# A sine table in 16-bit integers, a reciprocal by logarithm and exponential, and a reordered program

## The chip, the core and the metric

The kernel runs on one core of a Trainium2 chip. The metric is the device time of one execution in microseconds (us). The engines are PE (TensorE, matmuls, with its weight loads shown apart as PEld), DVE (VectorE), ACT (ScalarE), POOL (GpSimd) and SP (SyncE, which here issues all DMAs). Each engine takes its instructions in order; an instruction waits until what it reads is written and what it overwrites has been read.

## The reference

Two independent blocks on bf16 inputs of 2048 rows and 576 columns, whose results stand side by side in the output:

```python
# A: short filter, gate, long convolution over the sequence, gate
k_shift = sum_t k_pad[:, t:t+S, :] * shift_k[:, ks-1-t]      # ks = 4 taps
kv = k_shift * v
y = irfft(rfft(pad(kv)) * rfft(pad(ssm_k)))[:S]              # per column, length 2*2048
a = q * (y + kv * ssm_D)
# B: linear attention, 32 heads of 18
q, k, v = split(x @ wqkv); pq, pk = phi(q), phi(k)           # phi(t) = t+1 if t>0 else exp(t), plus 1e-6
kv = einsum("bhsd,bhse->bhde", pk, v); z = sum_s pk
b = (einsum(pq, kv) / (einsum(pq, z) + 1e-6)) @ wo
out = concat([a, b], axis=-1)
```

## The kernel before

Block A does the long convolution as a two-stage Fourier transform on PE. The 576 columns go in five chunks (four of 128 and one of 64). For each chunk and for the filter (letter h) and the signal (letter u): `s1` multiplies by the 16 tables of the sine matrices `G` (unit names h1, u1; eight matmuls, tile Ch or Cu), a DMA transpose turns the result (ht, ut; tile Cth, Ctu), and `s2` does the 16-point stage (h2, u2; tiles T for the filter and SU for the signal). `prod` multiplies the two complex spectra (pX, pT) and adds up planes (pA, pS). Where pA or pS has the engine letter N, it is left out and the inverse stage `i1` does the sum by eight more matmuls per half. `i1` writes V, and `i2` applies the transposed tables `F` and the gate q. `conv` (cv) is the short filter with the gate v, ahead of u1. The filter rows first get D added into their first column (hd) and are then transposed (hT): by PE and an eviction (letter D or A), or, for chunks 3 and 4 before the change, by a copy (letters a and p: tile hp) and a DMA transpose.

Block B transposes x (xd: by PE, or by DMA with the letter T), computes phi(k) for 16 groups of 128 rows (k) and phi(q) transposed (q, qt), sums x against phi(k) (G, zs), folds wv and wo in (kv, M), and divides by the denominator: den computes it and its reciprocal `rden`, bc and bt spread it over the columns of phi(q), o and ol are the last product with the output's DMA.

Nothing schedules this at run time. A string `ORDER` lists some 260 units by hand or by search, in the order in which they are written; each unit emits instructions to several engines, and every engine runs its own in that order. The letters behind a unit's dots choose the engine of an eviction or elementwise operation (A, D, P), and the digits behind the slash choose the PSUM banks (four pairs, 0 to 3) and buffer slots. A matmul into a bank waits until the bank's last reader is done. At the start: `io` makes small constants, `ix` the index of the sine tables on DVE (mp for the sine, mc for the cosine), `sin` turns them into G on ACT, `wu` issues matmuls on zeros ("warm_ps") before any data is there, Wj spreads the four filter taps over 128 partitions by matmuls from a row of ones (tile W_ps), dl and dc bring D. The index of an element is the product of (4k - 1) and (16p + s), taken modulo 8192.

Of the kernel before, what the change touches and what calls it, by code (L numbers as in the profile page):

```python
# [37 lines left out]
k.15/3 u1.0.1.0.A/2 hT.2.D/21 u1.0.0.1.A/0 u1.0.0.0.A/3 ht.1.1/0 cv.1.1.DD xd.1.T/1 k.13/2 h2.1.1.1.A/11 cv.1.2.DD
h2.1.1.0.A/0 q.3.1/3 h2.0.0.1.A/21 h2.0.0.0.A/2 ut.0.0/0 cv.1.3.DDP hl.3/0 q.3.0/0 q.1.0/1 u2.0.0.0.A/03 k.6/2
ut.0.1/1 k.7/0 u2.0.0.1.A/3 pX.0.0.D/0 qt.1/1 u2.0.1.0.A/12 u2.0.1.1.D/0 k.5/3 u1.1.1.0.A/12 kl.1 pT.0.0.D k.12/1  # L40
pX.0.1.D/1 u1.1.0.1.A/0 k.14/2 u1.1.1.1.A/3 ht.1.0/0 ql.0/1 cv.2.0.D u1.1.0.0.A/0 pT.0.1.D k.4/1 cv.2.1.DD
h1.2.1.1.A/03 pS.0.1.D pA.0.0.P ut.1.1/1 h1.2.1.0.A/2 hd.3 pA.0.1.D q.1.1/0 h2.1.0.0.A/33 h2.1.0.1.A/2 G.1/10
# [5 lines left out]
h1.3.1.1.A/1 u2.2.0.0.D/10 u2.2.0.1.A/2 ut.2.1/0 i1.1.1.1.A/03 cv.4.0.D i1.1.1.0.A/1 cv.4.1.DD den/0 lwo ht.3.1/1
hT.4.p/20 u2.2.1.1.A/02 i1.1.0.1.A/3 i1.1.0.0.A/1 M.2.A/2 M.3.A/3 i2.1.1/1 h2.3.1.1.A/12 cv.4.2.PP u2.2.1.0.A/0
i2.1.0/3 pX.2.0.P/1 u1.3.1.1.A/01 bc.2/20 u1.3.0.1.A/3 u1.3.0.0.A/1 bt/2 pA.2.0.N u1.3.1.0.A/3 M.1.A/0 ht.3.0/0  # L50
h2.3.1.0.D/1 h2.3.0.1.A/32 bc.0/30 h1.4.1.0.A/11 h1.4.0.1.A/2 st.0 h2.3.0.0.A/1 ut.3.0/1 pT.2.0.P bc.3/32 h1.4.1.1.A/0
M.4.A/1 M.0.A/3 bc.1/01 h1.4.0.0.A/2 pS.2.0.P u2.3.0.0.A/13 u2.3.0.1.A/2 pX.2.1.P/0 ut.3.1/0 ht.4.0/1 ql.1/1 pT.2.1.D
# [21 lines left out]
def _warm(tc, psum, K, n):  # L74

    nc = tc.nc
    zero = K.sm[:, 1984:2048].bitcast(BF)
    ps = psum.tile([128, 4, 128], FP32, name="warm_ps")
    for _ in range({'A': 5, 'B': 8, 'C': 7, 'D': 6}[n]):
        nc.tensor.matmul(ps[:], lhsT=zero, rhs=zero.unsqueeze(1).to_broadcast([128, 4, 128]), start=True, stop=True)  # L80


# [33 lines left out]
def _small(tc, cpool, slot, K):  # L116
    nc = tc.nc
    K.sm = slot([128, 2048], FP32, "sm")
    nc.vector.memset(K.sm[:, 1984:2048].bitcast(BF), 0.0)
# [2 lines left out]
    nc.gpsimd.iota(K.sm[:, 256:272], pattern=[[1, 16]], base=0, channel_multiplier=16,
                   allow_small_or_imprecise_dtypes=True)
# [3 lines left out]
    nc.vector.memset(K.negpi[:], -math.pi)  # L127
# [8 lines left out]
def _dft_index(tc, slot, K, part, h):

    nc = tc.nc
    b = slice(8 * h, 8 * h + 8)
    if part == 0:  # L140
        kap = K.sm[:, 128:256].unsqueeze(1).to_broadcast([128, 8, 128])
        sv = K.sm[:, 256 + 8 * h:264 + 8 * h].unsqueeze(2).to_broadcast([128, 8, 128])
        if not hasattr(K, 'mp'):
# [1 line left out]
        nc.vector.tensor_tensor(out=K.mp[:, b], in0=kap, in1=sv, op=ALU.mult)
        nc.vector.tensor_single_scalar(out=K.mp[:, b], in_=K.mp[:, b], scalar=8191, op=ALU.bitwise_and)
    else:
        if not hasattr(K, 'mc'):
            K.mc = slot([128, 2, 16, 128], I16, "mc")
        nc.vector.tensor_single_scalar(out=K.mc[:, 0, b], in_=K.mp[:, b], scalar=6144, op=ALU.add)  # L150
        nc.vector.tensor_single_scalar(out=K.mc[:, 1, b], in_=K.mc[:, 0, b], scalar=8191, op=ALU.bitwise_and)


# [90 lines left out]
def kernel(  # L244
# [134 lines left out]

    def shift_w(eng='A'):  # L380
        one = K.sm[0:97, 769:833].bitcast(BF)
        for i, e in enumerate({'A': 'AAA', 'D': 'DDD', 'M': 'ADA', 'N': 'DAD'}[eng]):
            d0, dn = 256 * i, min(256, D - 256 * i)
            ps = psum.tile([128, 1024], FP32, name="W_ps")
            for c0 in range(0, 4 * dn, 512):
                c1 = min(c0 + 512, 4 * dn)
                nc.tensor.matmul(ps[:, c0:c1], lhsT=one, rhs=K.Srow[:, 4 * d0 + c0:4 * d0 + c1], start=True, stop=True)
# [328 lines left out]
    def b_den():  # L716
# [17 lines left out]
        nc.vector.tensor_scalar(out=den, in0=den, scalar1=ez[:, 0:1], scalar2=None, op0=ALU.add)  # L734
        with nc.allow_low_precision(reason="the reciprocal is used as bf16"):
            nc.vector.reciprocal(out=B['rden'], in_=den)
# [88 lines left out]


    UNITS = {
        'xl': load_x, 'wm': one_w, 'lw': load_w, 'ls': load_shift, 'lz': zero_rows, 'Wj': shift_w, 'eps': eps_col,
        'dl': load_D, 'dc': turn_D, 'id': lambda: _ident(tc, cpool, K), 'io': lambda: _small(tc, cpool, slotx, K),
        'ix': lambda p, h: _dft_index(tc, slotx, K, p, h), 'iv': lambda: _w16_phase(tc, K),  # L830
        'iw': lambda: _w16_index(tc, K), 'wk': lambda: _w16_mask(tc, K), 'sin': lambda ri, h: _sine(tc, cpool, K, ri, h),
# [57 lines left out]
```

## Time and profile before

| what | us |
|---|---|
| median of three runs | 161.43 (161.31 to 162.2) |
| profiled execution, span from its first to its last instruction | 159.3 |
| PE busy in it | 147.6 |
| DVE busy | 139.8 |
| ACT busy | 128.4 |
| POOL busy | 65.2 |

The runs are timed from outside, the span from inside the profile, so the median stands 2.1 us over the span; the time of the profiled execution around its span is not shown apart. Busy means that at least one instruction of the engine was running. The end of a matmul is modelled and matmuls are pipelined, so the distance between starts says more of PE's rate than a matmul's length. In the rows that follow, a line number such as L532 is that of the kernel before; "x16" is the number of instructions, and what stands in square brackets is the idle time ahead of them and what ended it.

### The profile page before, as it was taken

To read this page: it belongs to the slowest core of one execution; us is meant where nothing else is said; L and a number is where in the kernel's file an instruction comes from. 1 tells how busy PE (TensorE), PEld (TensorE's weight loads), DVE (VectorE), ACT (ScalarE), POOL (GpSimd) and SP (SyncE) were. 2 spreads that over 40 slices of the span, in tenths; PEclk is the share of its full clock that TensorE was granted. 3 is DMA by queue.
4 is the path that set the end of the run, shared out by engine and by line. 5 is a ranking of instruction groups with operands and counts; after the bars stand their busy time and mean duration, and the time that the engine had idled before them with its cause. 6 is when DMAs were issued, how large, how long until landed. Compare 5 with 4: busy or idle time off the path is not lost.

```text
span 159.3 us, 4563 instructions
## 1 busy us (share of the span) xinstructions
PE 147.6 (93%) x1966; PEld 92.2 (58%) x1982; DVE 139.8 (88%) x170; ACT 128.4 (81%) x157; POOL 65.2 (41%) x67
## 2 busy tenths in 40 slices
PE   6799999999999999999998999999878999998990
PEld 1498564465734467467466568576445565677550
DVE  7978699899899999999899989998999999998420
ACT  7979996899997999959996956997999685786331
POOL 7407541806510970008100019589997077400000
PEclk9999999999999999999999999999999999999999
DMA  3999999990979999999999999684999999444282
GB/s 105 352 368 294 255 239 305 152 231 3 164 130 228 243 228 240 189 212 312 159 196 272 242 155 212 187 141 90 268 152 184 175 324 204 124 117 136 62 264 100
DMA packets 74171, 31.92 MB, mean 200 GB/s; under 512 B 52074, under 2 KB 73509, under 8 KB 74150
## 3 DMA queue, kind: packets, MB, share of 16 engines
q1 hardware_dynamic: 74150, 31.62, 91.7%
q8 instruction: 15, 0.25, 0.7%
q14 instruction: 6, 0.05, 0.1%
HBM read 14.97 MB, written 4.72 MB: 124 GB/s over the span
## 4 chain that ended last, share of the span: by engine, by line
PE 66%; POOL 12%; DVE 8%; DMA 6%; issue 3%; ACT 3%; SPq 0%; DVEq 0%; ACTq 0%; POOLq 0%
PE k_ps L451 12%; PE q_ps L460 11%; PE g_ps L659 6%; PE o_ps L776 6%; PE s_ps L532 6%; POOL X L567 5%; PE s_ps L555 5%; DMA Cth<-Ch 4%; PE i_ps L589 3%; POOL T L569 3%; PE hT_ps L511 2%; DMA pqT<-in_A_shift_k_dram 2%; PE xT_ps L337 2%; PE i_ps L602 2%; PE qt_ps L468 2%
## 5 line engine op out<-in xcount | busy, mean ns | idle before, releaser
L451 PE MATMUL k_ps<-wqk,xT 128*128 128x512 bf16 (+1 forms) x154 | 21.3, 282 | 0.3
L532 PEld LDWEIGHTS <-G 128*128 128x128 bf16 x320 | 17.4, 98 | 3.7 <-issue 3.4
L299 ACT ACTIVATE Cu<-s_ps 128x1024 bf16<-128x1024 f32 (+1 forms) x18 | 16.9, 978 | 2.1 <-DMA Cth<-Ch 1.4
L460 PE MATMUL q_ps<-xT,wqk 128*128 128x512 bf16 x78 | 18.2, 379 | 0.1
L451 PEld LDWEIGHTS <-xT 128*128 128x128 bf16 x160 | 11.4, 98 | 10.5 <-issue 0.5
L299 ACT ACTIVATE Ch<-s_ps 128x1024 bf16<-128x1024 f32 (+1 forms) x17 | 15.0, 928 | 3.0 <-PE s_ps L532 2.7
L299 ACT ACTIVATE ob<-o_ps 128x576 bf16<-128x576 f32 (+1 forms) x12 | 7.5, 636 | 11.3 <-PE o_ps L768 5.1
L299 ACT ACTIVATE V<-i_ps 128x1024 bf16<-128x1024 f32 x16 | 15.7, 1034 | 1.0 <-PE i_ps L589 1.0
L659 PE MATMUL g_ps<-pk,x_sb 128*128 128x65 bf16 (+1 forms) x124 | 16.3, 283 | 0.2
L299 ACT ACTIVATE T<-s_ps 128x1024 bf16<-128x1024 f32 x16 | 15.7, 1027 | 0.5 <-POOL at L490 0.5
L490 DVE TENSOR_TENSOR at<-at 128x2048 bf16<-128x2048 bf16 (+1 forms) x13 | 14.9, 1143 | 0.7 <-POOL at L489 0.3
L489 DVE TENSOR_TENSOR at<-k,Wj 128x2048 bf16<-128x2048 bf16 (+1 forms) x13 | 14.8, 1136 | 0.4 <-POOL at L490 0.4
L776 PE MATMUL o_ps<-wo_M,pqT 128*128 128x64 bf16 (+1 forms) x108 | 13.8, 283 | 0.5 <-issue 0.5
L444 DVE SCALAR_TENSOR_TENSOR pk<-pk,k_ps 128x576 bf16<-128x576 bf16 x16 | 11.8, 751 | 2.7 <-ACT pk L443 2.6
L299 ACT ACTIVATE SU<-s_ps 128x1024 bf16<-128x1024 f32 x14 | 14.1, 1029 | 0.0
L659 PEld LDWEIGHTS <-x_sb 128*128 128x128 bf16 x128 | 8.4, 97 | 8.7 <-issue 1.1
L460 PEld LDWEIGHTS <-wqk 128*128 128x128 bf16 x80 | 7.5, 98 | 9.1 <-issue 1.1
L443 ACT ACTIVATE pk<-k_ps,neg 128x576 bf16<-128x576 f32 x16 | 11.6, 745 | 1.2 <-PE k_ps L451 0.9
L604 DVE TENSOR_TENSOR q<-i_ps,q 128x1024 bf16<-128x1024 f32 (+1 forms) x10 | 11.0, 1107 | 1.2 <-PE i_ps L603 1.2
L776 PEld LDWEIGHTS <-pqT 128*128 128x128 bf16 x112 | 7.4, 98 | 7.6 <-issue 0.9
L490 POOL TENSOR_TENSOR at<-at 128x2048 bf16<-128x2048 bf16 (+1 forms) x2 | 6.2, 3097 | 12.9 <-DVE at L489 12.9
L532 PE MATMUL s_ps<-v,G 128*128 128x128 bf16 (+1 forms) x160 | 10.5, 214 | 1.0 <-ACT Cu L299 0.4
(161 smaller groups left out, 349.1 us busy)
## 6 DMA issues: line engine op xcount, KB each, us to landing
x_sb<-in_B_x_dram SPq DMA_DIRECT2D x4, 576.0 KB, 4.7
h_sb<-in_A_ssm_k_dram SPq DMA_DIRECT2D x4, 512.0 KB, 5.1
out_dram<-ob SPq DMA_DIRECT2D x7, 288.0 KB, 3.3
k<-in_A_k_dram SPq DMA_DIRECT2D x1, 1280.0 KB
v<-in_A_v_dram SPq DMA_DIRECT2D x1, 1280.0 KB, 8.5
q<-in_A_q_dram SPq DMA_DIRECT2D x1, 1280.0 KB
wqk<-in_B_wqkv_dram SPq DMA_DIRECT2D x2, 576.0 KB, 7.6
k<-in_A_k_dram SPq DMA_DIRECT2D x1, 1024.0 KB
```

Source lines behind the costliest of these rows:

```text
L299: nc.scalar.activation(out=out, in_=in_, func=ACT.Copy)
L443: nc.scalar.activation(out=out_ap, in_=ps_ap, func=ACT.Exp, bias=K.neg1[0:n, :])
L444: nc.vector.scalar_tensor_tensor(out=out_ap, in0=out_ap, scalar=1.0, in1=ps_ap, op0=ALU.min, op1=ALU.max)
L451: nc.tensor.matmul(ps[:, n0:n1], lhsT=xT[r // 4][:, t, rr * 128:(rr + 1) * 128], rhs=wqk[:, t, D + n0:D + n1], start=(t == 0), stop=(t == 4))
L460: nc.tensor.matmul(ps[:, j, :], lhsT=wqk[:, t, 128 * c:128 * c + 128], rhs=xT[g][:, t, :], start=(t == 0), stop=(t == 4))
L489: on[0].tensor_tensor(out=t_, in0=kk[:, 3 - stage:19 - stage], in1=wb(stage), op=ALU.mult)
L490: on[1].tensor_tensor(out=a_, in0=a_, in1=t_, op=ALU.add)
L532: nc.tensor.matmul(ps[:, bi, 0:dc], lhsT=K.G[ri][:, b, :], rhs=xf(b), start=True, stop=True)
L555: nc.tensor.matmul(ps[q:q + 32, z, :], lhsT=K.W0[64 * z:64 * z + 64, x, :], rhs=Ct[64 * z:64 * z + 64, r, :, j, :], start=True, stop=True)
L604: nc.vector.tensor_tensor(out=qs, in0=ps[:, :, 0:dc], in1=qs, op=ALU.mult)
L659: nc.tensor.matmul(ps[:, n0:n1], lhsT=x_sb[:, r, f0:f0 + fn], rhs=pk[:, r, n0:n1], start=(r == 0), stop=(r == 15))
L776: nc.tensor.matmul(pss[i][:, n0:n1], lhsT=pqT[:, c, r * 128:(r + 1) * 128], rhs=B['M'][:, c, n0:n1], start=(c == 0 and not first), stop=(c ...
```

## The change

It has five parts.

1. The index of the sine tables is made in 16-bit integers. Row s = 0 comes from one 32-bit product, whose low half is taken; rows 1, 2 to 3, 4 to 7 and 8 to 15 come by adding a constant row to the rows before, so that the number of rows doubles each time. Four iotas on POOL make the constant rows.
2. The taps' matmuls read one row instead of 97, so that the other 96 need not be zeroed (unit lz goes).
3. The filter's chunks 3 and 4 are transposed by PE and evicted by ACT.
4. The reciprocal on DVE is replaced by ln and exp(-x) on ACT. A table set that has both is loaded where exp's was.
5. ORDER is another one: units stand in other places, several evictions, products, sums and filter steps change engines, and nine start-up matmuls stand where there were five.

```diff
-    for _ in range({'A': 5, 'B': 8, 'C': 7, 'D': 6}[n]):
+    for _ in range({'A': 5, 'B': 4}[n]):
...
+    nc.gpsimd.iota(K.sm[:, 256:257], pattern=[[0, 1]], base=0, channel_multiplier=16,
...
+    K.mul = K.sm[:, 1160:1416].bitcast(I16).rearrange("p (i k) -> p i k", i=4)
+    for i in range(4):
+        nc.gpsimd.iota(K.mul[:, i], pattern=[[4 << i, 128]], base=-(1 << i), channel_multiplier=0)
...
-        nc.vector.tensor_tensor(out=K.mp[:, b], in0=kap, in1=sv, op=ALU.mult)
-        nc.vector.tensor_single_scalar(out=K.mp[:, b], in_=K.mp[:, b], scalar=8191, op=ALU.bitwise_and)
+            m = slot([128, 2, 16, 128], I16, "mp")
+            K.ma, K.mp = m[:, 0], m[:, 1]
+        if h == 0:
+            first = K.sm[:, 840:968].bitcast(I32)
+            nc.vector.tensor_scalar(out=first, in0=K.sm[:, 128:256], scalar1=K.sm[:, 256:257], scalar2=None, op0=ALU.mult)
+            low = first.bitcast(I16).rearrange("p (k two) -> p k two", two=2)[:, :, 0]
+            nc.vector.tensor_single_scalar(out=K.ma[:, 0], in_=low, scalar=8191, op=ALU.bitwise_and)
+        for i in range(3) if h == 0 else (3,):
+            n = 1 << i
+            nc.vector.tensor_tensor(out=K.ma[:, n:2 * n], in0=K.ma[:, 0:n],
+                                    in1=K.mul[:, i].unsqueeze(1).to_broadcast([128, n, 128]), op=ALU.add)
+        nc.vector.tensor_single_scalar(out=K.mp[:, b], in_=K.ma[:, b], scalar=8191, op=ALU.bitwise_and)
...
+    nc.scalar.preload_act_table_set("natural_log_exp_and_others")
     nc.scalar.activation(out=K.warm[:], in_=K.neg1[:], func=ACT.Exp)
...
-    K.Srow = pqT[0:97].rearrange("o c n -> o (c n)")[:, 0:4 * D]
+    K.Srow = pqT[0:1].rearrange("o c n -> o (c n)")[:, 0:4 * D]
...
-    def zero_rows():
-        z = K.sm[0:96, 1984:2048]
-        nc.scalar.activation(out=K.Srow[0:96, :].bitcast(FP32).rearrange("p (a b) -> p a b", b=64),
-                             in_=z.unsqueeze(1).to_broadcast([96, 18, 64]), func=ACT.Copy)
...
-        nc.vector.tensor_scalar(out=den, in0=den, scalar1=ez[:, 0:1], scalar2=None, op0=ALU.add)
-        with nc.allow_low_precision(reason="the reciprocal is used as bf16"):
-            nc.vector.reciprocal(out=B['rden'], in_=den)
+        nc.scalar.activation(out=den, in_=den, func=ACT.Ln, bias=ez[:, 0:1])
+        nc.scalar.activation(out=B['rden'], in_=den, func=ACT.Exp, scale=-1.0)
...
-io dl ix.0.0/0 hl.0/0 lz sin.1.0 eps ix.1.0/1 id ls ix.0.1 iw ix.1.1 xl.2 sin.0.0 wk wu.1.A/0 lw.2 dc/1 hd.0 Wj.A/230
+xl.2 io wu.2.B/0 wu.1.A/1 wk dl ls ix.0.0/0 ix.0.1 ix.1.1/1 sin.1.0 sin.1.1 id dc/2 sin.0.1 wm hl.0/0 hd.0 ix.1.0
```

At three places the two orders read as follows. In each row stand the line, the operation, what is written and read, and the size; line numbers behind L490 are 5 higher after the change.

First, SP's queue from the loads of block A's filter input k on, until x's last group but one: before,

```order
L406 DMA k<-in_A_k_dram 112x3x256
L409 DMA k<-in_A_k_dram 128x16x256
L438 DMA h_sb<-in_A_ssm_k_dram 128x2048
L539 DMA_TRANSPOSE Cth<-Ch 128x16x128
L319 DMA x_sb<-in_B_x_dram 128x4x576
L409 DMA v<-in_A_v_dram 128x16x256
```

and after:

```order
L411 DMA k<-in_A_k_dram 112x3x256
L414 DMA k<-in_A_k_dram 128x16x256
L414 DMA v<-in_A_v_dram 128x16x256
L544 DMA_TRANSPOSE Cth<-Ch 128x16x128 x2
L443 DMA h_sb<-in_A_ssm_k_dram 128x2048
L329 DMA x_sb<-in_B_x_dram 128x4x576
L614 DMA_TRANSPOSE F_617<-G_133 128x16x128
```

The loads of v moved ahead, and h's third chunk and an x group moved behind both transposes of chunk 0.

Second, DVE around the denominator (den_ps; wo_M is the buffer that holds the reciprocal): before,

```order
L490 TENSOR_TENSOR at<-at 128x16x64
L732 TENSOR_SCALAR ez<-den_ps 128x1
L734 TENSOR_SCALAR den_ps<-den_ps,ez 128x512
L736 RECIPROCAL wo_M<-den_ps 128x512
L604 TENSOR_TENSOR q<-i_ps,q 128x8x128 x2
L746 SCALAR_TENSOR_TENSOR pqT<-pqT,bc_ps 128x1024 x2
```

and after:

```order
L495 TENSOR_TENSOR at<-at 128x16x64
L737 TENSOR_SCALAR ez<-den_ps 128x1
L577 TENSOR_TENSOR X<-X 128x2x512
L311 CAST wo_M<-m_ps 128x576
L609 TENSOR_TENSOR q<-i_ps,q 128x8x128 x2
L750 SCALAR_TENSOR_TENSOR pqT<-pqT,bc_ps 128x1024 x2
```

Two wide operations left this place and two shorter ones came.

Third, POOL from the clearing of wo_M on, to its last operation (T and X are the products of the spectra, "at" the short filter): before,

```order
L641 MEMSET wo_M 128x576
L572 TENSOR_TENSOR T<-T 128x2x512
L518 COPY hp<-h_sb 64x2048
L489 TENSOR_TENSOR at<-k,Wj 128x16x64
L490 TENSOR_TENSOR at<-at 128x16x64
L567 TENSOR_TENSOR X<-SU,T 128x2048
L569 TENSOR_TENSOR T<-SU,T 128x2048
L572 TENSOR_TENSOR T<-T 128x2x512
L567 TENSOR_TENSOR X<-SU,T 128x2048
```

and after:

```order
L646 MEMSET wo_M 128x576
L577 TENSOR_TENSOR T<-T 128x2x512
L492 TENSOR_TENSOR at<-k,Wj 128x16x64
L574 TENSOR_TENSOR T<-SU,T 128x2048
L577 TENSOR_TENSOR T<-T 128x2x512
L572 TENSOR_TENSOR X<-SU,T 128x2048
L494 TENSOR_TENSOR at<-k,Wj 128x16x64
```

The copy hp, one product X and one filter step left the place ahead of the second X, and a filter step moved behind it.

More of the change, by code (lines that the diff above doesn't have):

```diff
@@ L38 @@
[L38 to L42, printed above, removed]
@@ L48 @@
[L48 to L52, printed above, removed]
@@ new lines @@
+h1.3.0.0.D/1 ut.2.1/1 M.2.A/0 i1.1.0.1.A/03 pS.1.1.P u2.2.1.0.D/12 i1.1.0.0.A/0 i1.1.1.0.A/1 cv.4.0.P ht.3.1/0
+i1.1.1.1.A/3 u2.2.1.1.A/2 pX.2.0.D/0 pT.2.0.P pS.2.0.P cv.4.1.DD den/0 pA.2.0.D M.3.D/1 ht.3.0/1 i2.1.0/3 h2.3.1.1.A/32
+i2.1.1/1 h1.4.1.0.A/00 u1.3.1.1.A/13 bc.2/20 u1.3.0.1.A/1 u1.3.0.0.A/3 bt/2 u1.3.1.0.A/1 h1.4.1.1.A/0 h2.3.1.0.D/3
+h1.4.0.0.A/2 h1.4.0.1.D/1 h2.3.0.1.A/20 bc.0/23 h2.3.0.0.A/1 M.4.A/0 M.1.A/2 bc.3/10 M.0.A/3 ut.3.0/0 u2.3.0.1.A/02
+u2.3.0.0.A/1 bc.1/30 ht.4.0/1 ut.3.1/0 i1.2.0.1.A/02 st.0 ql.1/0 pX.2.1.P/1 i1.2.0.0.A/1 h2.4.0.1.A/13 pT.2.1.D pS.2.1.N
@@ new lines @@
+cv.4.2.PD cv.4.3.DDD o.0.2.DA/20 pX.3.0.D/0 pA.2.1.P i1.2.1.1.A/1 o.1.2.AAf/30 u1.4.0.0.D/11 u1.4.1.0.A/2 h2.4.0.0.D/3
+u1.4.0.1.A/0 pT.3.0.D u1.4.1.1.A/1 ut.4.0/1 i1.2.1.0.A/2 pS.3.0.D u2.3.1.1.A/10 u2.3.1.0.A/3 i2.2.1/1 o.1.0.AA/20
+pX.3.1.D/1 pA.3.1.D o.0.0.AAf/31 pA.3.0.P i1.3.0.1.A/12 pT.3.1.D u2.4.0.0.A/00 u2.4.0.1.D/3 pS.3.1.P i2.2.0/1 st.1
+i1.3.0.0.A/2 pX.4.0.D/0 pA.4.0.D pT.4.0.D i1.3.1.0.A/3 i1.3.1.1.A/0 o.1.3.DAs/12 i2.3.1/3 i2.3.0/0 pS.4.0.N
+i1.4.0.0.A/02 i1.4.0.1.A/1 i2.4.1/3 i2.4.0/0 st.2 o.1.1.AD/23 o.0.3.DDs/10 ol.0.1/231
@@ L149, in _dft_index @@
             K.mc = slot([128, 2, 16, 128], I16, "mc")
-        nc.vector.tensor_single_scalar(out=K.mc[:, 0, b], in_=K.mp[:, b], scalar=6144, op=ALU.add)
+        nc.vector.tensor_single_scalar(out=K.mc[:, 0, b], in_=K.ma[:, b], scalar=6144, op=ALU.add)
         nc.vector.tensor_single_scalar(out=K.mc[:, 1, b], in_=K.mc[:, 0, b], scalar=8191, op=ALU.bitwise_and)
@@ L367 @@
     pk = big.tile([128, 16, D + 1], BF, name="pk", tag="pk")
-    K.Srow = pqT[0:97].rearrange("o c n -> o (c n)")[:, 0:4 * D]
+    K.Srow = pqT[0:1].rearrange("o c n -> o (c n)")[:, 0:4 * D]
     def load_shift():
-        nc.vector.memset(K.sm[0:97, 769:833].bitcast(I32), 0x3F803F80)
-        nc.sync.dma_start(out=K.Srow[96:97, :], in_=A_shift_k.rearrange("(o d) j -> o (d j)", o=1))
-    def zero_rows():
-        z = K.sm[0:96, 1984:2048]
-        nc.scalar.activation(out=K.Srow[0:96, :].bitcast(FP32).rearrange("p (a b) -> p a b", b=64),
-                             in_=z.unsqueeze(1).to_broadcast([96, 18, 64]), func=ACT.Copy)
+        nc.vector.memset(K.sm[0:1, 769:833].bitcast(I32), 0x3F803F80)
+        nc.sync.dma_start(out=K.Srow, in_=A_shift_k.rearrange("(o d) j -> o (d j)", o=1))
     def shift_w(eng='A'):
-        one = K.sm[0:97, 769:833].bitcast(BF)
+        one = K.sm[0:1, 769:833].bitcast(BF)
         for i, e in enumerate({'A': 'AAA', 'D': 'DDD', 'M': 'ADA', 'N': 'DAD'}[eng]):
@@ L827 @@
     UNITS = {
[L828 removed]
+        'xl': load_x, 'wm': one_w, 'lw': load_w, 'ls': load_shift, 'Wj': shift_w, 'eps': eps_col,
         'dl': load_D, 'dc': turn_D, 'id': lambda: _ident(tc, cpool, K), 'io': lambda: _small(tc, cpool, slotx, K),
```

33 lines of the change are left out of this document (14 added, 19 removed).

## The prediction

> **What bounds the kernel now.** I read the page first (busy shares and slices), then busy time by stretches, then the chain of waits in the stretches that show idle time, then single groups for prices.
>
> ```profile
> PE 147.6 (93%) x1966; PEld 92.2 (58%) x1982; DVE 139.8 (88%) x170; ACT 128.4 (81%) x157; POOL 65.2 (41%) x67
> PE   6799999999999999999998999999878999998990
> DVE  7978699899899999999899989998999999998420
> ```
>
> TensorE (PE) and VectorE (DVE) are both near full for almost the whole span. The stretches say which is the limit where:
>
> ```profile
> 24.00:80.00 56.00, 55.58 (x623) 30.86 (x629) 52.99 (x54) 50.16 (x58) 20.24 (x8) 1.00 1.02 198
> 80.00:122.00 42.00, 38.86 (x640) 25.93 (x642) 40.80 (x50) 35.30 (x42) 24.44 (x9) 1.00 0.99 196
> 122.00:148.00 26.00, 24.70 (x451) 17.05 (x447) 24.37 (x28) 18.67 (x24) 8.93 (x4) 1.00 0.74 170
> ```
>
> The columns after the length are busy us of PE, weight loads, DVE, ACT, POOL, then granted clock. From 24 to 80 us PE is idle for 0.4 us: there only less PE work or an earlier start helps. From 80 to 122 us PE idles 42.00 - 38.86 = 3.1 us while DVE is busy 40.80 of 42 (97%): there DVE and what it waits for set the pace. From 122 to 148 us PE idles 1.3 us. The chain of waits of the middle stretch does not run through PE at all:
>
> ```profile
> 103.92 2.13 POOL at L489
> ...
> 108.25 4.04 POOL X L567
> ...
> 118.62 4.04 POOL X L567
> ...
> 122.68 1.23 DVE T L569
> ```
>
> From 103.92 to 122.66 GpSimd (POOL) works without a gap on six operations (two filter steps of the last chunk, three products, one subtraction), and DVE's next product waits for the last.
>
> **The start.** In the chain of waits from the first DMA:
>
> ```profile
> 1.64 3.38 DMA pqT<-in_A_shift_k_dram
> ...
> 5.15 2.08 PE W_ps L387 x5
> 7.23 1.71 PE hT_ps L511 x16
> 8.94 1.52 PE xT_ps L337 x16
> ...
> 12.81 1.08 PE hT_ps L511 x16
> 13.88 0.89 PE xT_ps L337 x16
> ...
> 15.00 0.22 PE k_ps L451
> ...
> 23.39 0.45 PE s_ps L532 x8
> ```
>
> The same sixteen transposes take 1.71 and 1.52 us before 10.5 us and 1.08 and 0.89 us after it, at a granted clock that the stretches give as 1.00: PE reaches full rate only some 5 us after its unbroken work begins at 5.15. The change puts nine start-up matmuls where five were. By the rows below the five began at 1.06 and were over at 3.37, and PE then stood nearly idle until 5.15; nine last until about 5.0 (4 more at about 0.42, the spacing of the five W_ps), so work is unbroken from 1.06 and full rate should come at about 6 to 7 us, before hT and xT. ScalarE (ACT) bounds the same place from the other side:
>
> ```profile
> 1.06 2.31 PE L80 MATMUL warm_ps<-sm 128*128 128x512 bf16 x5 [1.06 <-DVE negpi L127]
> 3.28 1.15 ACT L222 ACTIVATE G<-mp,negpi 128x1024 bf16<-128x1024 int32 x1
> 6.20 2.22 ACT L299 ACTIVATE Wj<-W_ps 128x1024 bf16<-128x1024 f32 x3 [0.18 <-PE W_ps L387]
> ```
>
> **The change, part by part.** Prices of the removed operations:
>
> ```profile
> L736 DVE RECIPROCAL wo_M<-den_ps 128x512 bf16<-128x512 f32 x1 | 3.4, 3358 | 0.0
> L145 DVE TENSOR_TENSOR mp<-sm 128x1024 int32<-128x1024 f32 x2 | 2.4, 1192 | 0.2 <-POOL sm L122 0.2
> L146 DVE TENSOR_SCALAR mp<-mp 128x1024 int32<-128x1024 int32 x2 | 1.4, 694 | 0.1
> L490 DVE TENSOR_TENSOR at<-at 128x1024 bf16<-128x1024 bf16 x2 | 1.4, 692 | 0.1
> L150 DVE TENSOR_SCALAR mc<-mp 128x1024 int16<-128x1024 int32 x2 | 1.4, 688 | 0.0
> L734 DVE TENSOR_SCALAR den_ps<-den_ps,ez 128x512 f32<-128x512 f32 x1 | 0.8, 758 | 0.1
> L151 DVE TENSOR_SCALAR mc<-mc 128x1024 int16<-128x1024 int16 x2 | 0.9, 426 | 0.1
> L516 ACT ACTIVATE hp<-h_sb 128x2048 bf16<-128x2048 bf16 x1 | 4.0, 4006 | 0.0
> L299 ACT ACTIVATE xT<-xT_ps 128x2048 bf16<-128x2048 bf16 x1 | 1.9, 1871 | 0.0
> L443 ACT ACTIVATE pq<-qt_ps,neg 128x512 bf16<-128x512 f32 x2 | 1.4, 690 | 0.0
> ```
>
> 1. *Index.* Before: 2 x (1.19 + 0.69 + 0.69 + 0.43) = 6.0 us of DVE. After: six 1024-wide 16-bit scalar operations at 0.43 = 2.6; one 1024-wide 16-bit addition between 0.69 (bf16 of that size) and 1.19 (the 32-bit multiply), I take 0.69, the row of its width; five small ones, at most 0.69 each and above nothing, estimated at 1.4 together. Sum 4.7, so 1.3 us less on DVE (between 0.7 more and 2.7 less). Four more iotas on POOL lie beside this. First sine at about 3.1 instead of 3.28; but three sines (1.15 each) now stand ahead of the h column and the Wj evictions on ACT, where two stood, so these evictions start at about 7.0 instead of 6.20. The zeroing of the other 96 rows leaves ACT; the W matmuls stream as many columns as before, so PE gains nothing from one row.
>
> 2. *Start, summed.* W 5.1 to 7.0; hT 1.08, to 8.1; xT 0.89 once the first Wj bank is out (8.0), its second piece after the second bank, to 9.3; two of the first-stage h units (0.45 each) to 10.2; the next hT needs a bank that ACT empties at about 10.2 (Wj until 9.2, then two short operations), to 11.4; one unit, to 11.8; xT of group 0, to about 13.0. Then the first k at 13.0 instead of 15.0, with one 0.45 unit put off: 1.5 us gained. With slow transposes up to the old time of 10.5 it is about 0.5. The x load now goes out ahead of the shift row and both h loads, some 0.4 us each, which also pulls to the low side. I take 1.0.
>
> 3. *PE work.* Chunks 3 and 4 of the filter are transposed by PE (16 + 16 matmuls: 1.08 + at most 1.08, 1.9 taken) instead of by DMA. The inverse stage loses 48 matmuls; their spacing is 2.34 / 80 = 29 ns, so 1.4 us:
>
> ```profile
> 73.56 2.34 PE i_ps L589 x80
> ```
>
> Net 0.5 us more, and PE has no slack to hide it in. ACT loses the 4.0 us copy hp and gains 1.87 and about 1.0 of evictions; POOL loses a copy of about the same size; two DMA transposes go. The transpose of the first sine plane is issued much earlier, far ahead of its use, for nothing.
>
> 4. *Reciprocal.* DVE loses 0.76 + 3.36 = 4.1 us inside the stretch where it is 97% busy. ACT gains two passes over 128x512, 1.4 us by the row of the same size. The Trainium skill ("ScalarE: Activation LUTs", Table sets: the hidden batching unit) says that the set natural_log_exp_and_others holds both ln and exp; no trace of before shows it, and without such a set its 2.7 us per switch would, as an estimate, add 5 us to ACT here. Behind den PE has products of the inverse and forward stages before the first broadcast, as before, so ACT's lateness is covered up to some 3 us.
>
> 5. *Sides of evictions, products and filter steps.* Counted by unit: seven 1024-wide evictions go from DVE to ACT, six come (-1.2), the rest (M, output, products, sums) +3.0, so DVE gains 1.8 and over the whole kernel loses 4.1 + 1.3 - 1.8 = 3.6 us. POOL's unbroken run gets shorter: one 4.04 product and one filter step of 2.13 leave the middle of it, so its last X is ready up to 6 us sooner relative to its inputs. Both limits of the 80 to 122 stretch are eased; up to 3.1 us of PE idle can go. PE itself then is the limit, and evictions by ACT are late next. I take 2.0 of the 3.1.
>
> 6. *Late stage.* The last inverse step of chunk 4 lost its neighbour: in the order before, an i2 of chunk 3 (0.9 us) stands between i1 and i2 of chunk 4, and PE still waits there:
>
> ```profile
> 147.21 0.19 PE L602 MATMUL i_ps<-V,F 128*128 128x64 bf16 x1 [0.59 <-ACT V L299]
> ```
>
> After, nothing stands between: the wait becomes up to 1.5 us. Against it the i2 fills PE earlier and DVE has less to do after 122 us. I take 0 (from -1.0 to +0.9). The final outputs keep their form: 0.
>
> Sum: -1.0 + 0.5 - 2.0 = -2.5 us on a span of 159.3, 156.8. The shown runs have a median of 161.43, 2.1 over the span of the profiled one; with this added, about 159.0.
>
> **Rivals.** (a) *All idle goes.* Start 1.5, all 3.1 us, +0.5: -4.1, 157.3. For it: DVE and POOL are both eased; against: PE is 92% busy there and some waits are PE's own issue.
> (b) *Relief does not reach PE.* Start 0.5, +0.5, and 0.5 of the idle: 160.9. For it: ACT takes the logarithm and more evictions there, and PE, in order, waits for whichever eviction is last.
> (c) *A new wait for transposed data, the slower side.* The fourth first-stage unit of chunk 0 is put off until after the first k's, and the DMA transposes of chunk 0 wait for it on SP; behind them on that queue stand the loads of h chunk 2 and x group 3. Rows of the queue and of PE's cover:
>
> ```profile
> 14.54 5.75 SPq L539 DMA_TRANSPOSE Cth<-Ch  x1
> ...
> 20.96 0.58 SPq L409 DMA_DIRECT2D v<-in_A_v_dram  x1
> 21.58 7.77 SPq L539 DMA_TRANSPOSE Cth<-Ch  x1
> ...
> 31.69 2.91 SPq L539 DMA_TRANSPOSE Cth<-Ch  x1
> ```
> ```profile
> 34.96 2.16 PE q_ps L460 x10
> 37.12 1.23 PE k_ps L451 x10
> ```
>
> By the sums above that unit leaves ACT at about 24 us; PE needs its transposes after two q, two k and two units (7.7 us) at about 30, and x group 3 at about 39. If the two transposes hold the queue 7.8 us each, x is there at 24 + 15.6 + 5 = 44.6, 5.5 us late: 164.5. It decides from about 5 us each; at 6.5 it is 162.0. Against it: the 7.8 stood right behind the v load, which now goes out before, and the 2.9 stood behind none.
> (d) *The clock rises later.* Extra start-up matmuls buy nothing if full rate comes at 10 us as before: the start is 0.5, and the time 159.5. The Trainium skill ("TensorE: Matmul & The Clock Gate", The HAM clock gate) has the rate follow a free-running window of 3.4 us, and elsewhere on that page says that transposes do not count as busy; the trace, where the rate rose amid transposes three microseconds after the last true matmul, leaves the second in doubt.
>
> **Chances.** A measurement here tells some 0.5% (0.8 us) from no change. My case with (d), 0.45, between 158.0 and 160.4; (a) 0.21; (b) 0.20, of it a quarter on the faster side; (c) 0.14, of it a sixth below the slower bound. Faster 0.45 + 0.21 + 0.04 = 0.70, slower 0.12 from (c) and 0.02 from (b), same 0.16. The range reaches below (a) to 156.3 and to the cheaper end of (c), 162.0.
>
> **What would show it.** First k at 13 to 14.5 us and transposes of 1.0 us at 7 us (step 2); no wait of PE for Cth or x near 30 to 39 us (c); PE idle from 80 us to the last broadcast down from 3.1 to about 1 us and no gapless POOL run ahead of DVE's product (4, 5); ACT's two passes at 0.7 us with no table load beside them (4); PE waiting about 1.5 us for V near the end (6). The prediction is wrong if PE's idle moves to ACT's evictions instead, or if the DMA queue holds PE in the first 40 us.

## The result, and the profile after

The change made the kernel slower by an eighth: 181.93 us in the median of four runs (180.85 to 182.31) against 161.41 (161.31 to 162.2), a ratio of 1.126 with a 95% interval from 1.120 to 1.131. The forecast was 159.0, with a range from 156.3 to 162.0. The profiled execution has a span of 180.2 us against 159.3: 20.9 us to be found.

The page of the changed kernel: busy times, then PE, POOL and the granted clock in forty slices.

```profile
PE 157.3 (87%) x1970; PEld 96.0 (53%) x1970; DVE 147.2 (82%) x174; ACT 127.2 (71%) x159; POOL 64.5 (36%) x71
PE   7799999998995599999999899709888984999693
POOL 7235617072379024090033181899600220400000
PEclk9969999999999699999999999996999998589998
```

DVE was to lose 3.6 us and shows 7.4 more than before. PE has holes (5 5, 7 0) where it had none, and after each the clock, which was 9 throughout, falls to 5 or 6. The same stretches as in the prediction:

```profile
24.00:80.00 56.00, 51.54 (x515) 27.68 (x516) 48.88 (x47) 43.68 (x52) 23.83 (x9) 0.97 0.85 176
80.00:122.00 42.00, 35.51 (x586) 24.07 (x579) 41.03 (x47) 31.03 (x40) 18.03 (x8) 0.99 0.92 171
122.00:148.00 26.00, 23.29 (x356) 14.97 (x354) 23.36 (x24) 21.16 (x27) 9.24 (x4) 0.95 0.61 139
```

From 24 to 80 us, where PE idled 0.4 us before and where I expected no change, it idles 4.5; from 80 to 122 us it idles 6.5 instead of 3.1, though DVE is "busy" 41.0 of 42. What PE waited for (engine and line that waits, releaser, us in total, times, longest):

```profile
PE i_ps L607 <- DVE wo_M L311: 3.9, 1, 3.9
PE k_ps L456 <- DVE pqT L449: 3.7, 1, 3.7
PE o_ps L772 <- DVE q L609: 2.6, 1, 2.6
PE s_ps L560 <- DMA Cth<-Ch: 2.0, 2, 1.5
PE i_ps L607 <- ACT V L309: 2.0, 2, 1.4
```

The first two follow from one and the same thing. These are rows of DVE and of POOL (start, duration) at the two places, first 54 us, then 114 us; the last row of each list is a third place, at 94 us:

```profile
54.30 4.96 DVE L498 TENSOR_TENSOR v<-at,v 128x2048 bf16<-128x2048 bf16 x1
114.16 4.36 DVE L495 TENSOR_TENSOR at<-at 128x1024 bf16<-128x1024 bf16 x1
118.51 2.53 DVE L577 TENSOR_TENSOR X<-X 128x1024 bf16<-128x1024 bf16 x1
94.08 3.15 DVE L494 TENSOR_TENSOR at<-k,Wj 128x2048 bf16<-128x2048 bf16 x1
```
```profile
53.78 4.40 POOL L572 TENSOR_TENSOR X<-SU,T 128x2048 bf16<-128x2048 bf16 x1 [1.35 <-ACT SU L309]
113.53 4.44 POOL L574 TENSOR_TENSOR T<-SU,T 128x2048 bf16<-128x2048 bf16 x1 [4.66 <-DVE X L572]
118.05 2.44 POOL L577 TENSOR_TENSOR T<-T 128x1024 bf16<-128x1024 bf16 x1
93.05 3.10 POOL L577 TENSOR_TENSOR X<-X 128x1024 bf16<-128x1024 bf16 x1 [11.87 <-DVE ex L654]
```

DVE's product v takes 4.96 us where the same form took 1.22; it starts 0.5 us after POOL's product and ends 1.1 us after it. The half-wide sum "at" takes 4.36 instead of 0.69 and ends 0.55 us after POOL's. With one more at 94 us (3.15 instead of 1.22), the four take 11.2 us longer than their forms did before (3.74 + 1.93 + 3.67 + 1.85). Without them DVE would be busy 136.0 us. They count as busy, and what is queued behind them on DVE is what PE waits for: the pqT operation at 59 us and the eviction of M (wo_M L311) at 121 us. The trace of before held the sign, in rows that I had not read. (POOL's list for the kernel before, ahead of the prediction, stops at the second X at 118.58 us; three more operations follow it, and the second row here is one of them.)

```profile
133.93 1.68 DVE L567 TENSOR_TENSOR X<-SU,T 128x2048 bf16<-128x2048 bf16 x1
132.41 2.13 POOL L572 TENSOR_TENSOR X<-X 128x1024 bf16<-128x1024 bf16 x1
```

1.68 instead of 1.22, beside a POOL operation that ends at 134.54. The order before let this happen in two places, for 0.6 us in all.

The third wait comes from SP's queue (SPq; the q load's own wait is 5.9 us for the store ahead of it):

```profile
131.78 1.83 SPq L544 DMA_TRANSPOSE Cth<-Ch  x1
134.30 1.88 SPq L544 DMA_TRANSPOSE Ctu<-Cu  x1
136.23 1.05 SPq L828 DMA_DIRECT2D out_dram<-q  x1
143.22 0.59 SPq L414 DMA_DIRECT2D q<-in_A_q_dram  x1
151.28 1.23 DVE L609 TENSOR_TENSOR q<-i_ps,q 128x1024 bf16<-128x1024 f32 x1 [4.28 <-DMA q<-in_A_q_dram]
```

The first store now stands behind the transposes of chunks 3 and 4 and goes at 136.23 (at 110.9 before); the second half of q needs its buffer, so the load goes at 143.22 and DVE stands 4.28 us.

Last, the clock. PE busy is the second number of a row, the granted clock the third from the end:

```profile
56.25:59.67 3.42, 0.50 (x10) 0.21 (x9) 3.42 (x2) 1.60 (x3) 1.93 (x1) 1.00 1.08 298
59.67:63.08 3.41, 2.63 (x13) 1.24 (x13) 1.99 (x3) 0.04 (x1) 0.00 (x0) 0.50 0.97 287
5.06:8.47 3.41, 2.43 (x27) 1.56 (x27) 2.44 (x7) 3.07 (x6) 0.47 (x4) 1.00 0.98 363
8.47:11.88 3.41, 3.39 (x33) 3.39 (x33) 2.84 (x6) 2.15 (x5) 0.41 (x1) 0.50 1.08 326
```

There are five half-rate windows of 3.41 us before the last store: one each at 8.5, 59.7 and 121.1 us and two from 151.8. Ahead of each stretch of them stands a window in which PE idled. The reverse does not hold: from 165.49 to 168.90 us PE was busy only 1.99 us, and the next window ran at full rate. PE was busy 3.4, 2.6, 2.7 and 6.1 us in the half-rate windows, so by estimate about half of 14.8, 7.4 us, is lost; 1.7 of it lies at the start, where the kernel before lost time as well (first k at 15.00 us there, at 14.82 here).

The first four waits of the list (12.2 us) and these 7.4 us are the largest terms, but their sum is no difference of the two traces, since the kernel before has waits too. As a difference, PE idles 22.9 us instead of 11.7 and is busy 157.3 instead of 147.6, which gives the 20.9.

### The profile page after: what moved, and what is told of

Same layout as the page of the kernel before. It is cut to its first block, busy times and chain, and to the rows that moved or that the text cites. A ratio compares the mean times of both kernels' runs of the same rounds, so it can differ in the third digit from the quotient of the medians.

```text
span 180.2 us, 4564 instructions
## 1 busy us (share of the span) xinstructions
PE 157.3 (87%) x1970; PEld 96.0 (53%) x1970; DVE 147.2 (82%) x174; ACT 127.2 (71%) x159; POOL 64.5 (36%) x71
## 4 chain that ended last, share of the span: by engine, by line
PE 44%; DVE 31%; DMA 15%; ACT 4%; issue 3%; SPq 1%; DVEq 0%; ACTq 0%
PE k_ps L456 9%; DVE at L495 7%; PE s_ps L537 6%; PE q_ps L465 6%; PE o_ps L780 6%; DVE at L494 5%; DMA q<-in_A_q_dram 4%; DMA out_dram<-q 4%; DVE pqT L750 4%; DMA Cth<-Ch 4%; DVE v L498 3%; DMA h_sb<-in_A_ssm_k_dram 3%; PE s_ps L560 2%; PE g_ps L664 2%; DVE pqT L449 2%
## 5 line engine op out<-in xcount | busy, mean ns | idle before, releaser
L456 PE MATMUL k_ps<-wqk,xT 128*128 128x512 bf16 (+1 forms) x160 | 22.8, 295 | 3.7 <-DVE pqT L449 3.7
L495 DVE TENSOR_TENSOR at<-at 128x2048 bf16<-128x2048 bf16 (+1 forms) x15 | 20.4, 1361 | 0.5
L494 POOL TENSOR_TENSOR at<-k,Wj 128x2048 bf16<-128x2048 bf16 (+1 forms) x4 | 14.6, 3662 | 14.0 <-issue 7.4
L309 ACT ACTIVATE V<-i_ps 128x1024 bf16<-128x1024 f32 x18 | 17.4, 1024 | 3.0 <-PE i_ps L594 2.7
L309 ACT ACTIVATE Ch<-s_ps 128x1024 bf16<-128x1024 f32 (+1 forms) x18 | 16.7, 954 | 3.6 <-PE s_ps L537 3.5
L780 PE MATMUL o_ps<-wo_M,pqT 128*128 128x512 bf16 (+1 forms) x112 | 16.8, 308 | 0.3 <-ACT V L309 0.3
L577 POOL TENSOR_TENSOR X<-X 128x1024 bf16<-128x1024 bf16 x3 | 7.3, 2448 | 25.8 <-DVE X L572 13.9
L577 POOL TENSOR_TENSOR T<-T 128x1024 bf16<-128x1024 bf16 x4 | 8.8, 2202 | 21.6 <-DVE T L574 21.5
L664 PE MATMUL g_ps<-pk,x_sb 128*128 128x512 bf16 (+1 forms) x128 | 16.5, 286 | 0.0
L448 ACT ACTIVATE pk<-k_ps,neg 128x576 bf16<-128x576 f32 x16 | 11.7, 743 | 6.0 <-PE k_ps L456 5.7
L607 PE MATMUL i_ps<-V,F 128*128 128x128 bf16 (+1 forms) x80 | 9.6, 223 | 5.9 <-DVE wo_M L311 3.9
```

The source lines that it names most:

```text
L309: nc.scalar.activation(out=out, in_=in_, func=ACT.Copy)
L448: nc.scalar.activation(out=out_ap, in_=ps_ap, func=ACT.Exp, bias=K.neg1[0:n, :])
L456: nc.tensor.matmul(ps[:, n0:n1], lhsT=xT[r // 4][:, t, rr * 128:(rr + 1) * 128], rhs=wqk[:, t, D + n0:D + n1], start=(t == 0), stop=(t == 4))
L494: on[0].tensor_tensor(out=t_, in0=kk[:, 3 - stage:19 - stage], in1=wb(stage), op=ALU.mult)
L495: on[1].tensor_tensor(out=a_, in0=a_, in1=t_, op=ALU.add)
L577: e.tensor_tensor(out=a[:, :, 0, :], in0=a[:, :, 0, :], in1=a[:, :, 1, :], op=ALU.subtract if key == 'S' else ALU.add)
```

## Experiments

**The order or the code?** The changed kernel has new code (16-bit index, one-row W, ln and exp) and a new order. Each was run with the other's old half.

```diff
 e1: the changed kernel
-ORDER = the new one
+ORDER = the one before, without lz      # chunks 3 and 4 turned by DMA, five start-up matmuls
 e2: the kernel before
-ORDER = the one before
+ORDER = the new one, with lz            # nine start-up matmuls
```

> The changed kernel's code (16-bit index, one-row W, nine start-up matmuls, ln/exp reciprocal) in the order of the kernel before, with its sides and filter engines; the filter chunks are transposed as before. Theory 'the order costs': time near the kernel before, 158.5 to 161.5 us, granted clock 1.00 after the start, no DVE product of two SBUF inputs over 2 us. Rival 'the code costs' (the new index, W or reciprocal): 175 us or more.

> The code of the kernel before (32-bit index, full W, DVE reciprocal) in the order of the changed kernel. Theory 'the order costs': 178 to 186 us, with the same long DVE products (3 to 5 us) beside POOL's. Rival 'the code costs': under 165 us.

Measured: e1 162.71 us (ratio 1.009, 1.005 to 1.013), e2 184.66 (181.34 to 186.80). No ratio is given for e2, since its runs scatter; its lowest is still 12% above the kernel before, and its trace has the same four held operations of DVE (4.97, 3.15, 4.36 and 2.28 us). The order costs the eighth; the code by itself costs 0.9%. As the edit says, e1 has five start-up matmuls and not the nine of its expectation. That it missed its expected 158.5 to 161.5 is taken up below.

**Does POOL hold DVE?** In the two traces, lateness of an input cannot be told from a held instruction. A small kernel measures the pair by itself.

```diff
+for beside in (0, 1):
+    for s in ('two', 'long', 'psum', 'stt', 'cast', 'one'):
+        vector: a <- a product that waits for the phase before
+        if beside: gpsimd: g <- a * b      # 128x2048
+        vector: one cast from PSUM
+        kind(s); if beside: kind(s)
```

> A kernel of its own that computes nothing of the reference. First TensorE alone: 48 matmuls of 128x512, 240 transposes, 48 matmuls, a wait of about 5 us, 48 matmuls. Then six VectorE operations, each alone and then twice while GpSimd multiplies 128x2048 (4.07 us): a product of two SBUF tensors 1024 and 2048 wide, a product with one PSUM input, the (x+eps)*y operation with one PSUM input, a cast from PSUM, and a one-input 16-bit operation in SBUF. Theory 'shared port': the two-input SBUF products end 0.5 to 1.2 us after GpSimd's operation and take up to 4 to 5 us, those with a PSUM input and the cast keep 0.7 to 1.2 us; the 16-bit one is open (0.43 or up to 4). Rival 'late inputs or an overloaded VectorE': all keep their times of 0.68, 1.22, 1.21, 1.21, 1.21 and 0.43. TensorE: if transposes keep the clock up, all 240 take 56 ns each; if they count as idle, a stretch of 3.4 us or more of them runs at about twice that.

DVE's rows, first alone, then (x2) beside POOL: product 1024 wide, product 2048 wide, product with a PSUM input, 16-bit operation with one input.

```profile
59.44 0.68 DVE L73 TENSOR_TENSOR e<-c,f 128x1024 bf16<-128x1024 bf16 x1
62.44 1.21 DVE L75 TENSOR_TENSOR e<-c,f 128x2048 bf16<-128x2048 bf16 x1
76.41 0.42 DVE L83 TENSOR_SCALAR m<-n 128x1024 int16<-128x1024 int16 x1
79.01 4.35 DVE L73 TENSOR_TENSOR e<-c,f 128x1024 bf16<-128x1024 bf16 x2
85.55 5.41 DVE L75 TENSOR_TENSOR e<-c,f 128x2048 bf16<-128x2048 bf16 x2
93.15 2.47 DVE L77 TENSOR_TENSOR e<-pf,f 128x1024 bf16<-128x1024 f32 x2
109.32 3.82 DVE L83 TENSOR_SCALAR m<-n 128x1024 int16<-128x1024 int16 x2
114.18 1.22 DVE L75 TENSOR_TENSOR e<-c,f 128x2048 bf16<-128x2048 bf16 x1
```
```profile
78.05 4.05 POOL L90 TENSOR_TENSOR g<-a,b 128x2048 bf16<-128x2048 bf16 x1 [76.89 <-DVE a L69]
114.34 4.96 POOL L100 TENSOR_TENSOR g<-a,b 128x2048 bf16<-128x2048 bf16 x1 [1.96 <-DVE a L69]
```

Two products of 0.68 take 4.35 us: the first starts at 79.01 and the pair ends at 83.36, 1.3 us after POOL's end at 82.10, about the time of the two alone. Nothing of it went on beside POOL. The 16-bit operation with one SBUF input waits as well (3.82 for two of 0.42); the product with an input from PSUM does not (2.47 for two of 1.22), nor do the (x+eps)*y operation with one PSUM input (2.46 for two of 1.21) and the cast from PSUM (2.47 for two of 1.22). In the last pair DVE's product began 0.16 us first: it keeps its 1.22, and POOL takes 4.96 instead of 4.05. So whoever comes second waits for the whole of the other's operation. The Trainium skill ("SBUF — State Buffer", Who interferes with whom) says just this of a port pair that the two engines share: DVE contends when both inputs are in SBUF or in its two-port modes, and "Issue order, not op shape, decides who blocks". The trace agrees in all these cases, though no row says in which mode the 16-bit operation ran; I had not drawn on that page.

**Repairs.** Four operations from POOL to DVE (e3), the store ahead (e4), both with a fifth operation (e5).

```diff
 e3: the changed kernel's ORDER
-pX.0.0.P   pA.1.0.P   pT.2.0.P   pS.2.0.P
+pX.0.0.D   pA.1.0.D   pT.2.0.D   pS.2.0.D
 e4: the changed kernel's ORDER
-ut.3.0 ... ht.4.0 ut.3.1 ... st.0 ql.1
+st.0 ut.3.0 ... ht.4.0 ut.3.1 ... ql.1
 e5: e3 and e4, and
-pX.2.1.P
+pX.2.1.D
```

> The changed kernel with four operations moved from POOL to DVE: the two filter steps, the product and the subtraction beside which DVE's products took 2.5 to 5.0 us instead of 0.7 to 1.2. DVE gets 3.8 us more work and should lose 11.2 us of stretched time. Theory 'DVE is held by POOL's running operation, and PE by DVE': 168 to 174 us, the two PE waits of 4 us near 56 and 117 us gone. Rival 'the long products are late inputs, DVE is simply overloaded there': 182 us or more, since DVE has more to do.

> The changed kernel with the first output store put ahead of the last three transposes of the queue, nothing else. Theory 'the store behind them holds the q load, and that PE': 177 to 179.5 us, PE's waits before the output matmuls near 149 us (2.6 to 2.9 us) gone. Rival 'that wait is passed on to the last V and DVE': 181 to 182 us, the same as the changed kernel.

> The changed kernel with five operations moved from POOL to DVE (the four of before and the product that had slid into the place of one of them, +1.2 us for DVE beyond the four) and the first store ahead of the last three transposes. Theory 'ports first, store second': 170 to 174 us, both PE waits of over 4 us (near 111 and near 145 us) gone, one or no clock drop after 15 us. Rival 'the order is overloaded on DVE whatever the ports': 176 us or more.

Measured: e3 176.22 us (ratio 1.087, 1.079 to 1.094), e4 180.96 (1.122, 1.114 to 1.131), e5 170.22 (1.054, 1.049 to 1.058). DVE got more work in e3 and the time fell by 3.9% of the kernel before, so the held operations were on the path; but it did not reach the expected 168 to 174. Of the two waits of PE that were to go, the one for pqT went and the one for wo_M stayed, at 4.1 us. Two rows of e3 say why: the next POOL product in the queue, which starts 6.9 us after the moved one in the changed kernel, slid into its place and held the same sum on DVE.

```profile
110.54 4.35 DVE L495 TENSOR_TENSOR at<-at 128x1024 bf16<-128x1024 bf16 x1
109.87 4.47 POOL L572 TENSOR_TENSOR X<-SU,T 128x2048 bf16<-128x2048 bf16 x1 [6.67 <-ACT SU L309]
```

That product is the fifth move of e5. The store alone is not to be told from no change (its rival): the 2.6 us at the output went, and the wait for wo_M grew from 3.9 to 5.3 us. With the five operations moved as well, e5 is 11.7 us under the changed kernel and PE's two long waits on DVE and the one for q are gone. What the fifth move and the store give each was not taken apart, and two operations of DVE are still held in e5 (2.61 and 1.70 us, at 130.8 and 139.0 us).

**The remaining 8.7 us.** Four more kernels on top of e5: the transpose of the first sine plane later (e6), four evictions from DVE to ACT (e7), two more POOL operations on DVE (e14), filter chunks 3 and 4 turned by DMA again (e15).

```diff
 e6
-... FT.1.T k.3 ...          FT.0.T
+... k.3 ...                 FT.1.T FT.0.T
 e7
-u2.2.1.0.D  M.3.D  h2.3.1.0.D  h1.4.0.1.D
+u2.2.1.0.A  M.3.A  h2.3.1.0.A  h1.4.0.1.A
 e14
-pA.2.1.P  pA.3.0.P
+pA.2.1.D  pA.3.0.D
 e15
-hT.3.A  hT.4.A
+hT.3.a  hT.4.p
```

> The kernel with five operations moved to DVE and the first store ahead (170.2 us), and the transpose of the first sine plane moved on the queue from ahead of chunk 1's first transpose to beside the second plane's. Theory 'that transpose holds chunk 1's' (my rival of a wait on the queue in the first 40 us): the transpose of Cth starts near 33 to 36 us right at its data, PE's wait of 0.5 to 1.1 us near 42 to 43 us goes, 168.9 to 169.8 us. Rival 'Cth is late by DVE's and PE's own work': 170.0 to 170.6.

> The kernel with five operations moved to DVE and the first store ahead (170.2 us), with four evictions of its stretch from 100 to 125 us (M of chunk 3, one Cu, two Ch) moved from DVE to ACT. In that kernel DVE is busy 38.0 of the 40 us from 100 to 140 and PE idles 7.0 there. Theory 'what is left above the kernel before is DVE's load in that stretch': DVE loses some 3.3 us, 167 to 168.5 us. Rival 'the order of the chunks there (PE waits for transposes by DMA and for POOL) sets it': 169.7 to 171, no change.

> The kernel with five operations moved to DVE and the first store ahead (170.2 us), with two more of POOL's subtractions or sums moved to DVE, those beside which DVE's products still take 2.6 and 1.7 us (near 130 and 139 us). Theory 'ports still cost there': 168 to 169.3 us, PE's wait of 1.6 us for POOL's X near 131 us gone. Rival 'the order of the chunks sets that stretch': 169.8 to 171.

> The same kernel (170.2 us) with filter chunks 3 and 4 turned by DMA behind copies of ACT and POOL, as in the kernel before, instead of by PE. Theory 'the turning by PE costs in this order what it cost in the order before (2.9 us)': 167 to 168.5 us. Rival 'it fills waits here': 170 to 172 us, later for the copies.

Measured: e6 171.19 (1.061, 1.056 to 1.066), e7 171.42 (1.057, 1.049 to 1.064), e14 173.81 (1.074, 1.066 to 1.082), e15 178.24 (1.107, 1.099 to 1.114). None helped. In three of them PE's list of waits names what took the place, e6, e14 and e15 in turn:

```profile
PE i_ps L607 <- DMA F<-G: 1.4, 1, 1.4
```
```profile
PE i_ps L594 <- DVE X L577: 4.6, 1, 4.6
```
```profile
PE i_ps L607 <- DMA F<-G: 6.6, 1, 6.6
```

In e6 the short wait for chunk 1's Cth went, as its theory said, but the sine plane F is needed at 97.5 us and comes late when its transpose stands later, and later still behind the DMA transposes of the filter: the PE transposes had made room on that queue. The sum X that POOL gave up stands behind four filter operations in DVE's queue. In e7, DVE's busy time from 100 to 140 us fell from 38.0 to 33.8 of 40, and PE's stayed (33.0 and 32.9). Relief of DVE alone does not bring the rest back; but ACT took the evictions over, and PE's list has a new wait of 1.0 us for one of them (bc_ps for Ch), so DVE's load is not excluded as a part of it. In e6, e14 and e15 the repair is undone by the next dependence. The 8.7 us have no single cause that these runs show; that stays open.

**The single terms, in the old order.** Nine start-up matmuls (e8), ln and exp (e9), chunks 3 and 4 turned by PE (e12), each alone in the kernel before; and all the code with nine start-up matmuls (e10, that is e1 with nine).

```diff
 e8: the kernel before
-range({'A': 5, ...
+range({'A': 9, ...
 e9: the kernel before
-vector: den + ez; reciprocal
+scalar: ln(den + ez); exp(-x)
 e12: the kernel before
-hT.3.a  hT.4.p
+hT.3.A  hT.4.A
 e10: e1
-range({'A': 5, ...
+range({'A': 9, ...
```

> The kernel before with nine start-up matmuls instead of five and nothing else. My step on the start: full clock at 6 to 7 us, transposes of 1.0 us, the first k at about 13.5 us, and 159.5 to 160.5 us in all. Rival 'a later drop takes it back' (as the changed kernel's trace has it): a half-rate stretch after the gap between W and hT, first k at 14.5 to 15, 161 to 162 us.

> The kernel before with its DVE addition and reciprocal replaced by ln and exp on ACT, nothing else. Theory of my steps 4 and 5 (DVE is the limit there): DVE loses 4.1 us, ACT gains 1.3, PE's first broadcast comes 1 to 2 us earlier and the time is 159.4 to 160.8. Rival 'the chain there runs through POOL': 161.0 to 161.8, no change.

> The kernel before with filter chunks 3 and 4 turned by PE (evicted by ACT) instead of by DMA behind copies of ACT and POOL; nothing else. My step 3: PE +1.9 us (two times sixteen transposes), ACT -2 us, POOL -3.9 us of copies. If PE bounds there: 162.8 to 163.6 us. Rival 'the copy on POOL stands in the way of its products near 104 us, and the transposes fill PE's waits': 160.0 to 161.5 us.

> The changed kernel's code in the order of the kernel before (162.7 us with five start-up matmuls) with nine of them. Theory 'its loss against the kernel before is the clock's start' (first k at 15.6 us against 15.0): first k at 14.3 to 14.8, 160.3 to 161.2 us. Rival 'its loss is elsewhere (16-bit index, one-row W)': 162 us or more.

Measured: e8 160.02 us (ratio 0.989, 0.985 to 0.992), e9 162.39 (1.002, 0.999 to 1.005), e12 164.38 (1.019, 1.015 to 1.023), e10 161.13 (0.998, 0.996 to 1.001). PE's rows of e8 at the start:

```profile
7.11 1.15 PE L511 MATMUL hT_ps<-ident,h_sb 128*128 128x128 bf16 x16
8.10 1.06 PE L337 MATMUL xT_ps<-ident,x_sb 128*128 128x128 bf16 x16
```

Full rate from 7.1 us on, and the first k at 14.08 instead of 15.00. Of the parts run alone this is the one that pays, and e8 is the fastest of all kernels here. In e9 DVE was relieved as forecast, by 4.0 us over the whole kernel (in the stretch from 40.80 to 34.95), and PE did not gain; the chain of waits now runs through ACT, whose two passes stand ahead of the evictions SU and V that PE waits for:

```profile
80.00:122.00 42.00, 37.44 (x599) 25.04 (x598) 34.95 (x46) 34.61 (x41) 23.22 (x9) 1.00 1.04 188
```
```profile
103.31 1.84 ACT V L300 x2
105.16 0.66 ACT den_ps L735
105.84 0.60 ACT wo_M L736
106.44 0.91 ACT SU L300
107.35 1.84 ACT V L300 x2
```

In e12 both transposes lie whole on the chain (1.16 at 77.67 and 1.14 at 105.47), and PE waits another 1.3 us for the banks that they use (ACT's V): above 1.9, the term that I had given them. The time of e12 rose by 2.9 us, the median span of its runs by 2.3.

With nine matmuls e10 is back at the time of the kernel before, as its theory said, but that does not make the start the loss of e1. Nine matmuls gain 1.1% with the new code (1.009 to 0.998) as they do without it (0.989), so the code costs 0.9% either way. The first k of e10 comes at 13.82 us, 1.2 before that of the kernel before, and the kernel ends no sooner. Which part of the code costs the 0.9% stays open; ln and exp alone (e9) cost 0.2%, not to be told from nothing.

## Why the prediction was wrong, by its steps

- **Step 5 failed, and with it the forecast.** It priced moved operations by their duration alone and took the run of POOL's operations for a delay of what reads them. It did not ask which DVE operations run beside them. The order before puts two-input products beside POOL nearly nowhere; the new one does so in four places, for 11.2 us on DVE. Its count of the work was about right: DVE was to fall by 3.6 us to 136.2, and without the 11.2 us it would be busy 136.0. Moving five operations from POOL to DVE, together with the store, brings back 11.7 of the 20.5 us; the other 8.7 us stay open.
- **The premise of steps 4 and 5 was wrong too.** "There DVE and what it waits for set the pace" from 80 to 122 us: e9 took 5.9 us of busy time from DVE in that stretch, and the time stayed the same, within 0.5%. A busy share of 97% did not make DVE the limit; the chain of waits, which ran through POOL, said so already. Rival (b), relief that does not reach PE, is what e9 and e10 show.
- **The prices of steps 1 and 4 held.** The 16-bit addition took 0.68 us (0.69 taken), the whole index 4.9 us of DVE (4.7 taken), and the two passes on ACT 0.7 and 0.6 with no table load beside them, by the rows below. Two smaller things did not hold: the first sine came at 3.59 us and not at 3.1, and the upper bound of step 1, 0.7 us more, leaves out its own upper price of the addition (with 1.19 it is 1.2).

```profile
118.68 0.66 ACT L739 ACTIVATE den_ps<-den_ps,ez 128x512 f32<-128x512 f32 x1 [3.21 <-DVE ez L737]
119.38 0.60 ACT L740 ACTIVATE wo_M<-den_ps 128x512 bf16<-128x512 f32 x1
```

- **Step 2, the start, was right where the order is the old one** (e8: 0.9 us at the first k by its trace, 1.0 taken; the time fell by 1.1%, nearly twice that, and what gives the rest is not shown) **and came to nearly nothing in the new one.** W ran at full rate, but h, now loaded after x, landed at 7.15 us, PE idled 0.9 us, and the next window was at half rate: first k at 14.8, not 13 to 14.5. I had put a price on x going first, not on the clock falling again.
- **Step 3** stood at 0.5. Its +1.9 for the transposes measured 2.3 to 2.9 by itself (span and time of e12); in the new order it cannot be taken out singly, since the DMA form holds the sine plane back (e15).
- **Step 6 was right**: a wait for V of 1.4 us by the list of waits, 1.5 forecast.
- **Rival (c)** did not come where it was put: the two transposes of chunk 0 held the queue for 4.65 us together, not 7.8 each, and PE waited for neither. Of the 2.0 us that PE waited for Cth, 0.5 fell at 43 us, for chunk 1, and 1.5 at 117 us. The larger wait on that queue, for q behind the first store, I had not seen: I followed the moved steps through the first 40 us of the queue and not to its end.
- **The sentence on what would make it wrong** named ACT's evictions and the first 40 us of the DMA queue. The first is where the gain of ln and exp went; neither is where the loss came from.
- **Rival (d)** is not borne out in the old order, where full rate came at 7.1 us (e8); in the new one the half-rate window ends at 11.9 us, so full rate did come late, by the clock falling again. The Trainium skill's rule that it quotes ("TensorE: Matmul & The Clock Gate", Part 4: PE-mode transpose), that transposes do not count as busy, is not borne out either: in the small kernel 240 transposes without a pause ran 56 ns apart for four windows at full rate. The matmuls that waited after an idle 3.3 us ran at a granted clock of 0.61 for the first 3.4 us.

```profile
18.12 13.56 PE L54 MATMUL pt<-ident,c 128*128 128x128 bf16 x240
45.33 1.01 PE L50 MATMUL pw<-a,b 128*128 128x512 bf16 x2 [3.29 <-DVE a L61]
45.30:48.70 3.40, 3.15 (x9) 1.28 (x10) 0.00 (x0) 0.00 (x0) 0.61 0.02 5
```

## What to carry to other kernels

Before an operation is moved to or from GpSimd, list what VectorE runs at that time: two operations on SBUF that each take little can cost the sum of both, counted as busy, and with it a wait on TensorE and a half-rate window behind that wait. Move one at a time and profile again, since the next operation in the queue slides into the free place. And an engine that is 97% busy is the limit only if the chain of waits runs through it: take a term of it out alone before building on its relief.

## What the runs showed of the hardware

One operation with a single SBUF input, in 16 bits at 0.42 us per 1024, waits for GpSimd just as two-input products do; an operation with one input in PSUM does not. At the start of the changed kernel PE was busy 2.43 of 3.41 us, with one pause of 0.9, and the next window came at half rate; near its end PE was busy only 1.99 of such a window, and the next came at full rate. So the busy share by itself does not decide, and what does is not settled by these runs. The length of those windows, 3.41 us, is the one that the Trainium skill gives ("TensorE: Matmul & The Clock Gate", What's actually happening: 4096 cycles, free-running), and the trace agrees.
